# Keys of batches 3 to 7 projected by float32r parts in the full array, with the list of works searched anew

## The chip, the cores and the metric

The kernel runs on one core of one Trainium2 chip. The metric is the device time of one execution in microseconds (us); lower is better. Engines are named as the profile names them: PE (TensorE, matrix products; PEld its weight loads), DVE (VectorE), ACT (ScalarE), POOL (GpSimd), SP (SyncE, whose queue issues the DMAs).

## What is computed

Linear attention with positive random features, and then one feed-forward layer pair over its output. Inputs are q, k, v of 8 batches, 8 heads, 576 tokens, head size 64, and omega of 128 x 64, all float32.

```python
def phi(x):                                   # x already scaled by D ** -0.25
    proj = np.einsum('bhsd,md->bhsm', x, omega)
    h = proj - np.sum(x * x, axis=-1, keepdims=True) / 2.0
    h = h - np.max(h, axis=-1, keepdims=True)
    return np.exp(h) / np.sqrt(m)
q_p, k_p = phi(q_s), phi(k_s)
kv = np.einsum('bhsm,bhsd->bhmd', k_p, v)
z = np.sum(k_p, axis=2)
num = np.einsum('bhsm,bhmd->bhsd', q_p, kv)
attn = num / (np.einsum('bhsm,bhm->bhs', q_p, z)[..., None] + 1e-06)
x = attn.transpose(0, 2, 1, 3).reshape(4608, 512)
h = x @ w_in                                  # 512 x 2048
g = np.maximum(h, 0.0) + np.log1p(np.exp(-np.abs(h)))
out = g @ w_out                               # 2048 x 512
```

## The kernel before, in words

The heads of a batch are handled in two groups of four ("quads"; the names carry batch, quad and first token tile, so `xk_5_0_0` holds keys of batch 5, quad 0, tiles 0 and 1). A quad's 576 tokens come in units: tiles 0 and 1, tiles 2 and 3 (128 tokens each), and a tail of 64 tokens. `plan_unit` describes the work of one unit of queries or keys: a DMA brings it in twice (transposed, `raw`, and by rows, `nat`), the rows are squared and summed (`squares`, `norms`), `raw` is projected on omega, the maximum over the features is taken, and the exponent is written to the tile `phk` or `phq`.

There are two ways to project. In the plain one (`project`, line 590) a token tile takes two float32 products, one for each half of the 128 partitions (two heads stand above one another, 64 partitions each); the profile shows each as two PE instructions of 64x128, so a unit of two tiles, four pairs of heads, is 16 instructions. The maximum (`maxima`, line 640) and the exponent (`exponent`, line 660) read the PSUM result itself. In the split one (`high` line 604, `low` line 608, `product` line 615) the tile is taken apart into two float32r values, a rounded one and what is left; both stand above one another in the tile `sp`, so that all 128 partitions are used, and one product against `omr`, which holds omega's two parts side by side (256 columns), gives all that is wanted. Its two column halves are then added: `first` (line 625) copies one from PSUM to `phk`, `second` (line 628) adds the other; `all_maxima` (line 632) and `exponents` (line 637) work on `phk` in SBUF.

Which way a unit goes is decided by `if q.b < SPLIT[...]`: before, the queries and the 64-token tails of batches 2 to 7 are split, and the keys of all batches are plain (the limit for keys is 9, and there are 8 batches).

The feed-forward part runs beside this, in blocks of 512 tokens (the first two of 256): for each of 16 slices of the hidden layer, twelve products into a PSUM bank `h` (lines 1149 to 1151), softplus in three ACT steps and one DVE step (lines 1155 to 1164), the split of the result into float32r parts `gh` and `gl` (lines 1168, 1172), and twelve products into the output banks `acc` (lines 1209 to 1211). The last two blocks are computed together with fewer products (line 1483).

The order of everything is written out by hand: `do` collects works with what they wait for and which buffers they take and give, `in_order` goes through the table `ORDER`, and each engine then executes its works in that order. An entry says which work comes next and on which of its engines it runs, where it has two (DVE or POOL for `low`, ACT or DVE for `high` and `first`). The planner's costs in `in_order`, `change` and `dma` pick among free buffers, and where they show PE idle, `with_fill` puts products that nobody reads (line 1665). The buffer `x` (raw units) and the buffer `sp` exist once each, for queries and keys together; two PSUM banks (`at`) take the projections of batches 2 to 7.

Of the kernel before, what the change touches and what calls it, by code (L numbers as in the profile page):

```python
# [19 lines left out]
P = 128  # L20
# [14 lines left out]
START = {"SP": 0.6, "ACT": 2.1, "PE": 3.4}  # L35
SLOW = 6.8
# [281 lines left out]
def change(old, new):  # L318

    if old == new:  # L320
        return 0.0
    return {("r", None): 0.2, ("c", None): 0.07, (None, "r"): 0.32, (None, "c"): 0.275}.get((old, new), 0.185)
# [1450 lines left out]
```

## Time and profile before

| | |
|---|---|
| time, median of 3 runs | 1002.87 us (1000.95 to 1003.2) |
| time of the profiled execution | 1000.96 us |
| its span, first to last instruction | 999.2 us |
| PE busy | 983.9 us, 98% of the span |
| DVE busy | 782.6 us, 78% |
| ACT busy | 662.6 us, 66% |
| POOL busy | 239.3 us, 24% |
| plain projections of keys, line 590 | 532 PE instructions, 42.4 us |
| split projections, line 615 | 242 PE instructions, 32.5 and 8.1 us |

A row of a timeline gives the start, the time taken, the engine, the line, the operation, the tiles written and read, the shapes and how many instructions were merged into it; in brackets stands how long the engine had been idle, and what ended that. PE's matmuls overlap in these rows: what a product costs is read from one start to the next, not from its own duration.

### The profile page before, as it was taken

To read this page: it belongs to the slowest core of one execution; us is meant where nothing else is said; L and a number is where in the kernel's file an instruction comes from. 1 tells how busy PE (TensorE), PEld (TensorE's weight loads), DVE (VectorE), ACT (ScalarE), POOL (GpSimd) and SP (SyncE) were. 2 spreads that over 40 slices of the span, in tenths; PEclk is the share of its full clock that TensorE was granted. 3 is DMA by queue.
4 is the path that set the end of the run, shared out by engine and by line. 5 is a ranking of instruction groups with operands and counts; after the bars stand their busy time and mean duration, and the time that the engine had idled before them with its cause. 6 is when DMAs were issued, how large, how long until landed. Compare 5 with 4: busy or idle time off the path is not lost.

```text
span 999.2 us, 17174 instructions
## 1 busy us (share of the span) xinstructions
PE 983.9 (98%) x5721; PEld 805.7 (81%) x5721; DVE 782.6 (78%) x2072; ACT 662.6 (66%) x1621; POOL 239.3 (24%) x220
## 2 busy tenths in 40 slices
PE   9899999999999999999999999999999999999998
PEld 8778888787878877887878787878788778788886
DVE  7999987788888887878788877877788757998710
ACT  7999986667666675756666766767666635766610
POOL 2353232102313122222232221413121221111100
PEclk9999999999999999999999999999999999999999
DMA  9965445343343424352433334333433131000002
GB/s 313 374 229 182 125 151 140 116 121 95 119 127 114 133 78 143 106 150 77 120 105 112 106 98 148 101 109 119 109 121 118 54 103 42 1 1 1 1 11 74
DMA packets 65920, 113.56 MB, mean 114 GB/s; under 512 B 18444, under 2 KB 39080, under 8 KB 65832
## 3 DMA queue, kind: packets, MB, share of 16 engines
q1 hardware_dynamic: 65672, 112.34, 35.6%
q8 instruction: 45, 0.74, 0.3%
q14 instruction: 43, 0.35, 0.1%
q10 hardware_dynamic: 160, 0.13, 0.1%
HBM read 85.41 MB, written 27.03 MB: 113 GB/s over the span
## 4 chain that ended last, share of the span: by engine, by line
PE 89%; ACT 6%; DVE 4%; issue 1%; DMA 0%; SPq 0%; DVEq 0%; ACTq 0%
PE acc L1209 13%; PE acc L1210 12%; PE acc L1211 12%; PE h L1149 10%; PE h L1150 9%; PE h L1151 9%; PE ppk L590 3%; PE xp L1078 3%; PE kt L756 3%; PE pb L1483 2%; PE ppq L615 2%; PE pc L1483 2%; PE pa L1483 1%; PE h L1326 1%; PE h L1324 1%
## 5 line engine op out<-in xcount | busy, mean ns | idle before, releaser
L1209 PE MATMUL acc<-wo,gh 128*128 128x512 f32 x512 | 204.7, 400 | 0.5 <-DVE xq L925 0.4
L1210 PE MATMUL acc<-wo,gh 128*128 128x512 f32 x512 | 200.3, 391 | 0.0
L1211 PE MATMUL acc<-wo,gl 128*128 128x512 f32 x512 | 199.7, 390 | 0.0
L1149 PE MATMUL h<-xh,wi 128*128 128x512 f32 (+1 forms) x512 | 189.7, 370 | 1.9 <-DVE u L1164 1.8
L1150 PE MATMUL h<-xl,wi 128*128 128x512 f32 (+1 forms) x512 | 186.4, 364 | 0.0
L1151 PE MATMUL h<-xh,wi 128*128 128x512 f32 (+1 forms) x512 | 185.8, 363 | 0.0
L1172 POOL TENSOR_TENSOR gl<-u,gh 128x512 fp32r<-128x512 f32 (+1 forms) x63 | 80.5, 1277 | 221.8 <-ACT gh L1168 119.5
L1209 PEld LDWEIGHTS acc<-wo,gh 128*128 128x128 f32 x512 | 96.2, 188 | 27.6 <-issue 7.3
L1155 ACT ACTIVATE u<-h 128x512 f32<-128x512 f32 (+1 forms) x128 | 70.2, 549 | 68.1 <-PE h L1151 56.2
L1149 PEld LDWEIGHTS h<-xh,wi 128*128 128x128 f32 x512 | 96.5, 189 | 21.3 <-DVE u L1164 3.4
L1211 PEld LDWEIGHTS acc<-wo,gl 128*128 128x128 f32 x512 | 96.1, 188 | 20.7
L1210 PEld LDWEIGHTS acc<-wo,gh 128*128 128x128 f32 x512 | 96.4, 188 | 16.9
L1151 PEld LDWEIGHTS h<-xh,wi 128*128 128x128 f32 x512 | 96.5, 188 | 15.6
L1150 PEld LDWEIGHTS h<-xl,wi 128*128 128x128 f32 x512 | 96.7, 189 | 14.0 <-DVE xl L1098 0.2
L1164 DVE SCALAR_TENSOR_TENSOR u<-h,u 128x512 f32<-128x512 f32 (+1 forms) x128 | 78.6, 616 | 25.2 <-ACT u L1161 24.7
L988 DVE CUSTOM_DVE_ANT_0 junk<-phq,zb 128x128 bf16<-128x128 f32 (+1 forms) x228 | 74.6, 327 | 13.2
L1158 ACT ACTIVATE u<-u 128x512 f32<-128x512 f32 (+1 forms) x128 | 74.4, 582 | 2.9
L1161 ACT ACTIVATE u<-u 128x512 f32<-128x512 f32 (+1 forms) x128 | 74.2, 582 | 2.6
L660 ACT ACTIVATE phk<-ppk,smk 128x128 f32<-128x128 f32 x230 | 63.5, 381 | 14.7 <-DVE smk L652 14.6
L637 ACT ACTIVATE phq<-phq,smq 128x128 f32<-128x128 f32 x194 | 60.7, 391 | 12.1 <-DVE smq L652 12.0
L1168 ACT CAST gh<-u 128x512 fp32r<-128x512 f32 (+1 forms) x87 | 48.8, 563 | 24.3 <-DVE u L1164 11.2
L997 POOL TENSOR_TENSOR phq<-phq,dnq 128x512 f32<-128x512 f32 (+1 forms) x31 | 33.8, 1095 | 127.2 <-DVE dnq L993 103.6
(220 smaller groups left out, 1857.9 us busy)
## 6 DMA issues: line engine op xcount, KB each, us to landing
xk<-kx SPq DMA_DIRECT2D x28, 512.0 KB, 4.0
xq<-qx SPq DMA_DIRECT2D x28, 512.0 KB, 3.6
fdq<-flq SPq DMA_DIRECT2D x28, 512.0 KB, 2.8
qq<-fdq SPq DMA_DIRECT2D x112, 128.0 KB, 3.0
rawi<-wi SPq DMA_DIRECT2D x16, 512.0 KB, 6.9
rawo<-wo SPq DMA_DIRECT2D x16, 512.0 KB, 8.2
out<-o SPq DMA_DIRECT2D x32, 256.0 KB, 2.1
v<-vv SPq DMA_DIRECT2D x14, 576.0 KB, 3.8
```

The source lines that it names most:

```text
L988: nc.vector.tensor_tensor_reduce(jk[r, c % jk.shape[1]], ph[r, c], q.zb[r, h], 1.0, 1e-6, ALU.mult, ALU.add, dn[r, 0, c : c + 1])
L1149: nc.tensor.matmul(b["h"], wh, xh[:, cc, t], start=cc == 0, stop=False)
L1150: nc.tensor.matmul(b["h"], wh, xl[:, cc, t], start=False, stop=False)
L1151: nc.tensor.matmul(b["h"], wl, xh[:, cc, t], start=False, stop=cc == NCC - 1)
L1155: nc.scalar.activation(b["u"], b["h"], AF.Abs)
L1158: nc.scalar.activation(b["u"], b["u"], AF.Exp, scale=-1.0)
L1161: nc.scalar.activation(b["u"], b["u"], AF.Ln, bias=1.0)
L1164: nc.vector.scalar_tensor_tensor(b["u"], b["h"], 0.0, b["u"], ALU.max, ALU.add)
L1172: (nc.vector if e == "DVE" else nc.gpsimd).tensor_tensor(b["gl"], b["u"], b["gh"].bitcast(F32), ALU.subtract)
L1209: nc.tensor.matmul(dst, gh, w2[fc][:, 0, c], start=start, stop=False, **kw)
L1210: nc.tensor.matmul(dst, gh, w2[fc][:, 1, c], start=False, stop=False, **kw)
L1211: nc.tensor.matmul(dst, gl, w2[fc][:, 0, c], start=False, stop=stop, **kw)
```

## The change

The limit for keys falls from 9 to 3, so the units of two full tiles of keys of batches 3 to 7 (five batches, two quads, two units: 20 units) take the split way that queries already take. The first batch's keys come in with fewer DMAs: for token tiles 1 to 4 the key columns and the value columns that stand behind them are one transfer of 772 columns instead of two of 512 (256 for the last tile) and 260. Four of the planner's costs are changed, and the table `ORDER` is replaced as a whole.

```diff
-START = {"SP": 0.6, "ACT": 2.1, "PE": 3.4}
-SLOW = 6.8
+START = {"SP": 0.65, "ACT": 2.1, "PE": 3.4}
+SLOW = 7.2
...
 ORDER = (
-    384, 386, 410, 434, 458, 482, 391, 506, 530, 554, 578, 604, 630, 388, 463, 414, 666, 394, 418, 442, 466, 702, 436,
...
+    384, 394, 386, 410, 434, 456, 415, 418, 440, 462, 437, 390, 392, 396, 398, 416, 400, 402, 478, 500, 522, 544,
...
-    return {("r", None): 0.2, ("c", None): 0.07, (None, "r"): 0.32, (None, "c"): 0.275}.get((old, new), 0.185)
+    return {("r", None): 0.08, ("c", None): 0, (None, "r"): 0.4, (None, "c"): 0.29}.get((old, new), 0.185)
...
-        return max(0.55 * n, size / 400e3)
+        return max(0.55 * n, 0.11 + size / 450e3)
...
-        alone = early and kind == "k" and not u and not q.qd
+        apart = early and kind == "k" and not u
+        alone = apart and not q.qd
         b = {}
+
+        cols = w if alone else 2 * w if kind == "q" or apart or not early else VW
...
-                b["cols"](slice(0, w if alone else 2 * w))
+                b["cols"](slice(0, cols))
...
-        if early and kind == "k":
-            b["lv"] = do("SP", dma(P * 4 * (VW - UW)), lambda: b["cols"](slice(UW, VW)), behind=ld, delay=DL)
+        b["lv"] = do("SP", dma(P * 4 * (VW - UW)), lambda: b["cols"](slice(UW, VW)), behind=ld, delay=DL) if apart else None
...
-        if q.b < SPLIT["t" if tail else kind]:
+        if q.b < (3 if kind == "k" and not tail else 2):
```

On PE, at the first keys of batch 5, the order before has a plain projection of tiles 0 and 1 as one group between two pieces of the feed-forward part (`acc` and `h`):

```order
L1211 MATMUL acc_4_0_5049<-wo4_901,gl_4_4_5308 128x512
L590 MATMUL ppk_5_0_0_0_5337<-omf_82,xk_5_0_0_5185 128x128
L590 MATMUL ppk_5_0_0_1_5338<-omf_82,xk_5_0_0_5185 128x128
L590 MATMUL ppk_5_0_0_0_5337<-omf_82,xk_5_0_0_5185 128x128
L590 MATMUL ppk_5_0_0_1_5338<-omf_82,xk_5_0_0_5185 128x128
L590 MATMUL ppk_5_0_0_0_5337<-omf_82,xk_5_0_0_5185 128x128
L590 MATMUL ppk_5_0_0_1_5338<-omf_82,xk_5_0_0_5185 128x128
L590 MATMUL ppk_5_0_0_0_5337<-omf_82,xk_5_0_0_5185 128x128
L590 MATMUL ppk_5_0_0_1_5338<-omf_82,xk_5_0_0_5185 128x128
L1149 MATMUL h_4_7_5351<-xh_79,wi7_998 128x512
L1150 MATMUL h_4_7_5351<-xl_80,wi7_998 128x512
L1151 MATMUL h_4_7_5351<-xh_79,wi7_998 128x512
```

and now, at the same keys (lines have moved down by 18 or 19):

```order
L1229 MATMUL acc_4_1_5133<-wo4_884,gl_4_4_5368 128x512
L634 MATMUL ppk_5_0_0_0_5449<-omr_86,spk_5_0_0_5352 128x256 x2
L634 MATMUL ppk_5_0_0_1_5454<-omr_86,spk_5_0_0_5352 128x256 x2
L1167 MATMUL h_4_7_5460<-xh_79,wi7_971 128x512
L1168 MATMUL h_4_7_5460<-xl_80,wi7_971 128x512
L1169 MATMUL h_4_7_5460<-xh_79,wi7_971 128x512
L1167 MATMUL h_4_7_5460<-xh_79,wi7_971 128x512
L1168 MATMUL h_4_7_5460<-xl_80,wi7_971 128x512
L1169 MATMUL h_4_7_5460<-xh_79,wi7_971 128x512
L634 MATMUL ppk_5_0_0_2_5478<-omr_86,spk_5_0_0_5352 128x256 x2
L634 MATMUL ppk_5_0_0_3_5484<-omr_86,spk_5_0_0_5352 128x256 x2
L1167 MATMUL h_4_7_5460<-xh_79,wi7_971 128x512
```

The eight plain products in one place (16 instructions in the profile) have become two groups of four products of 256 columns, with six products of the feed-forward part between them. Over the whole program `ppk` now has 106 plain products instead of 266 and 208 split ones instead of 48.

On DVE, the same unit has these rows before: the sum of squares (line 580), the two maxima from PSUM (line 640), and two short steps.

```order
L1022 STREAM_TRANSPOSE flq_4_0_2_5358<-phq_4_0_2_0_5104 128x8x4x32
L580 TENSOR_REDUCE smk_5_0_0_5378<-xk_5_0_0_5185 128x8
L640 TENSOR_REDUCE smk_5_0_0_5378<-ppk_5_0_0_0_5337 128x4
L640 TENSOR_REDUCE smk_5_0_0_5378<-ppk_5_0_0_1_5338 128x4
L647 SCALAR_TENSOR_TENSOR smk_5_0_0_5378<-smk_5_0_0_5378 128x8
L652 SCALAR_TENSOR_TENSOR smk_5_0_0_5378<-smk_5_0_0_5378 128x8
L1022 STREAM_TRANSPOSE flq_4_0_4_5399<-phk_4_1_4_1_5218 128x2x4x32
L1172 TENSOR_TENSOR gl_4_5_5404<-u_4_5_5265,gh_4_5_5370 128x512
```

Now DVE makes the low parts ahead of the products (line 627), and the sum of squares follows:

```order
L851 TENSOR_TENSOR s_4_1_5236<-s_4_1_5236,phk_4_1_4_0_5289 64x256 x2
L627 TENSOR_TENSOR spk_5_0_0_5352<-xk_5_0_0_5307,spk_5_0_0_5352 64x512 x2
L1006 ISA junk_78,dnq_4_0_2_0_5342<-phq_4_0_2_0_5238,zb_4_0_4833 128x128
L1006 ISA dnq_4_0_2_0_5342 128x1
L599 TENSOR_REDUCE smk_5_0_0_5359<-xk_5_0_0_5307 128x8
L1190 TENSOR_TENSOR gl_4_4_5368<-u_4_4_5280,gh_4_4_5366 128x512
```

and further down the four additions (line 647) and one maximum over all eight rows (line 651):

```order
L647 TENSOR_TENSOR phk_5_0_0_0_5475<-ppk_5_0_0_0_5449,phk_5_0_0_0_5475 128x256
L647 TENSOR_TENSOR phk_5_0_0_0_5475<-ppk_5_0_0_1_5454,phk_5_0_0_0_5475 128x256
L623 CAST spq_4_1_0_5487<-xq_4_1_0_5467 64x512
L647 TENSOR_TENSOR phk_5_0_0_0_5475<-ppk_5_0_0_2_5478,phk_5_0_0_0_5475 128x256
L647 TENSOR_TENSOR phk_5_0_0_0_5475<-ppk_5_0_0_3_5484,phk_5_0_0_0_5475 128x256
L1011 RECIPROCAL dnq_4_0_4_0_5382<-dnq_4_0_4_0_5382 128x2
L1040 STREAM_TRANSPOSE flq_4_0_2_5502<-phq_4_0_2_0_5238 128x8x4x32
L651 TENSOR_REDUCE smk_5_0_0_5359<-phk_5_0_0_0_5475 128x8
L1190 TENSOR_TENSOR gl_4_6_5518<-u_4_6_5437,gh_4_6_5516 128x512
L1015 TENSOR_TENSOR phk_4_1_4_1_5290<-phk_4_1_4_1_5290,dnq_4_0_4_0_5382 128x256
```

Two maxima have become two subtractions, four additions and one longer maximum; the units of keys now take turns with those of the queries, as `spq_4_1_0` between two additions shows. Counted over the program, DVE has 80 more additions for keys (line 647), 40 fewer maxima from PSUM and 20 more from SBUF, 28 more subtractions for keys and 13 fewer for queries; ACT has 69 more copies of `phk` (line 644), 32 more casts for keys and 11 more for queries (line 623); POOL has 12 more subtractions for keys and 13 more for queries.

On SP, the first weights now come after ten rows of the first batch's loads instead of eighteen; from token tile 1 on, a key transfer is half as large again, the separate transfers of 260 columns are gone but for tile 0, and the queries' loads follow the keys'.

## Rows read from the trace of the kernel before

**Rows 1.** The page: its busy times and the clock granted to PE.

```profile
PE 983.9 (98%) x5721; PEld 805.7 (81%) x5721; DVE 782.6 (78%) x2072; ACT 662.6 (66%) x1621; POOL 239.3 (24%) x220
...
PEclk9999999999999999999999999999999999999999
```

**Rows 2.** Busy time by stretch: start and end, then its length, engines, clock, DMA.

```profile
0.00:50.00 50.00, 45.04 (x384) 39.77 (x384) 43.47 (x155) 41.53 (x122) 15.65 (x24) 1.00 0.93 344
50.00:100.00 50.00, 46.77 (x383) 40.02 (x383) 49.00 (x123) 48.24 (x134) 23.85 (x18) 1.00 0.60 206
100.00:150.00 50.00, 49.29 (x382) 43.33 (x380) 44.91 (x135) 44.18 (x125) 15.74 (x16) 1.00 0.45 137
200.00:750.00 550.00, 549.37 (x3123) 442.53 (x3123) 441.07 (x1199) 367.19 (x896) 134.03 (x117) 1.00 0.38 114
```

**Rows 3.** The waits of PE: us in total, times, longest.

```profile
PE ppk L590 <- DMA xk<-k: 0.9, 2, 0.7
```

**Rows 4.** Timeline of PE around one plain unit, the first keys of batch 5.

```profile
434.10 0.39 PE L1211 MATMUL acc<-wo,gl 128*128 128x512 f32 x1
434.41 1.16 PE L590 MATMUL ppk<-omf,xk 64*128 64x128 f32 x16
435.50 0.50 PE L1149 MATMUL h<-xh,wi 128*128 128x512 f32 x1
435.84 0.39 PE L1150 MATMUL h<-xl,wi 128*128 128x512 f32 x1
```

**Rows 5.** Line 590 alone in the stretch of the 20 units.

```profile
200.00:750.00 550.00, 23.68 (x320) 19.70 (x320) 1.00 0.38 114
```

**Rows 6.** Timeline of all engines where split products run.

```profile
467.39 0.39 PE L1211 MATMUL acc<-wo,gl 128*128 128x512 f32 x1
...
467.62 0.64 PE L615 MATMUL ppq<-omr,spq 128*128 128x256 f32 x4
...
468.09 0.40 PE L1149 MATMUL h<-xh,wi 128*128 128x512 f32 x1
...
468.32 0.40 PE L1150 MATMUL h<-xl,wi 128*128 128x512 f32 x1
...
470.39 2.70 POOL L829 TENSOR_TENSOR s<-s,phk 128x512 f32<-128x512 f32 x2
...
470.77 2.61 DVE L608 TENSOR_TENSOR spk<-xk,spk 64x256 fp32r<-64x256 f32 x2
...
472.69 0.28 PE L615 MATMUL ppk<-omr,spk 128*128 128x256 f32 x1
...
473.44 0.38 PE L615 MATMUL ppk<-omr,spk 128*128 128x256 f32 x1 [0.47 <-DVE spk L608]
...
474.30 0.39 PE L1209 MATMUL acc<-wo,gh 128*128 128x512 f32 x1
```

**Rows 7.** Line 608: count, then ns min/median/max, first and last start.

```profile
L608 DVE TENSOR_TENSOR spk<-xk,spk x9: 418/420/1393, 150.8 to 743.7; 64x256 fp32r<-64x256 f32 x9
```

**Rows 8.** Timeline of PE at one more plain unit.

```profile
270.03 1.60 PE L590 MATMUL ppk<-omf,xk 64*128 64x128 f32 x16
```

**Rows 9.** Timeline of PE at 786 us.

```profile
786.12 0.47 PE L615 MATMUL ppq<-omr,spq 128*128 128x256 f32 x2 [0.57 <-DVE phq L628]
```

**Rows 10.** Groups by form: busy, mean ns of one, idle before.

```profile
L640 DVE TENSOR_REDUCE smk<-ppk 128x4 f32<-128x512 f32 x56 | 36.4, 682 | 9.2 <-PE ppk L590 8.7
...
L608 DVE TENSOR_TENSOR spq<-xq,spq 64x512 fp32r<-64x512 f32 x42 | 31.5, 749 | 3.0 <-ACT spq L604 1.9
...
L628 DVE TENSOR_TENSOR phk<-ppk,phk 128x256 f32<-128x256 f32 x24 | 9.4, 418 | 0.9 <-ACT phk L625 0.6
...
L632 DVE TENSOR_REDUCE smq<-phq 128x8 f32<-128x1024 f32 x24 | 29.2, 1217 | 0.6
...
L604 ACT CAST spq<-xq 64x512 fp32r<-64x512 f32 x28 | 17.3, 617 | 0.4
...
L625 ACT COPY phk<-ppk 128x256 f32<-128x256 f32 x17 | 5.8, 373 | 10.4 <-PE ppk L615 10.4
```

More of the change, by code (lines that the diff above doesn't have):

```diff
@@ L662, in plan_unit @@
         ld = do(
-            "SP", dma(P * 4 * (w if alone else 2 * w)) + (0.6 if early and u == q.qd == 1 else 0), load, behind=prev.get("load"),
+            "SP", dma(P * 4 * cols) + (0.7 if apart and q.qd else 0), load, behind=prev.get("load"),
             take=[("w" if early else "x", b, "x")], delay=DL, spare=2 if early else 0,
@@ L667, in plan_unit @@
         if alone:
-            prev["load"] = ln = do("SP", 0.75, lambda: b["cols"](slice(w, 2 * w)), behind=ld, delay=DL)
-        if early and kind == "k":
-            b["lv"] = do("SP", dma(P * 4 * (VW - UW)), lambda: b["cols"](slice(UW, VW)), behind=ld, delay=DL)
+            prev["load"] = ln = do("SP", 0.55, lambda: b["cols"](slice(w, 2 * w)), behind=ld, delay=DL)
+        b["lv"] = do("SP", dma(P * 4 * (VW - UW)), lambda: b["cols"](slice(UW, VW)), behind=ld, delay=DL) if apart else None
         s = do(("POOL", "ACT"), (pool(w), act(w)), squares, after=[ln])
```

491 rows, old and new, of the table ORDER are left out of this document.

## The prediction

> **What bounds the kernel now.** I read the page's busy times first [rows 1]: PE works for 98% of the span, at the full 2.4 GHz clock in every slice, and no other engine passes 78%. The stretches come next [rows 2]. In the first 50 us PE is idle for 5.0 us, in the second 50 for 3.2, in the third for 0.7; from 200 to 750 us, where all keys stand that change their way, it is idle for 0.6 of 550 us, with DVE at 441.07 / 550 = 80%, ACT at 67% and POOL at 24%. So in that stretch the time is PE's own work: what PE no longer has to do comes off the end one for one, as long as the other three still deliver in time. Busy time alone does not price a product, since matmuls overlap; so the third view is the timeline of PE, read from start to start.
>
> **The plain projection goes, 20 times.** The source has 5 batches, 2 quads and 2 full units each; line 590 shows x320 instructions in the stretch, 16 for each unit, so all 20 lie there [rows 5]. At one of them the last 512-column product ahead starts at 434.10 and the second one behind at 435.84, 1.74 us later [rows 4]. Without the group two products would have started in that time, 0.23 us each (467.39 to 467.62 in [rows 6]). The group costs 1.74 - 0.46 = 1.28 us. Some 0.2 us of it are the late starts at both edges (0.31 us ahead of the group and 0.34 behind the next product, where 0.23 is usual), which the full array does not show.
>
> **The split products come, 80 token tiles.** Two tiles in a row are four products of 256 columns: 467.39 to 468.32 is 0.93 us, less the same 0.46 is 0.47 us [rows 6]. A unit of four tiles takes 0.94 us. The order leaves most of them in such groups of two tiles, and a group by itself splits no further work. So a unit gives back 1.28 - 0.94 = 0.34 us, and 20 units 6.8 us. This is the one term that is nearly certain, since both kinds of group are in the trace of before, among the same neighbours.
>
> **What DVE, ACT and POOL get.** DVE: 80 additions at 418 ns are 33.4 us; 20 maxima over eight rows at 1217 ns are 24.3, against 40 maxima at 682 ns that go, 27.3; 28 subtractions for keys at 749 ns are 21.0, and 13 for queries that go to POOL are 9.7 less [rows 10]. Together +41.7 us, which lifts DVE from 80% to 483 / 550 = 88% of the stretch. ACT: 69 copies at 373 ns and 43 casts at 617 ns [rows 10] are 25.7 + 26.5 = 52.2 us, so 419 / 550 = 76%. POOL gets 25 subtractions more. All this lies beside PE's products; it costs nothing while the softplus steps and the queries' additions still come in time, and what they cost if they don't is the next term. A new wait comes with it: the buffer `sp` is one for queries and keys, so ACT's cast for the next unit waits for the last product of the one before, with softplus steps queued behind that cast on ACT; the order puts the casts behind such products.
>
> **Waits in the stretch.** Before, PE lost time there in two visible places: one plain group took 1.60 us instead of the usual 1.16, 0.44 lost [rows 8], and a run of split products, 472.69 to 474.30, took 1.61 where 0.47 is usual (467.62 to 468.09), 1.1 lost [rows 6]. A third stands just behind, 0.57 at 786.12 [rows 9]. That is 2.1 us, and as the whole order is new, those three go. How many come instead no row can say, so I bound it. The lower end is none at all, a gain of 2.1 us. The upper end is the rate of the stretch from 100 to 150 us, where DVE works for 44.9 of 50 us, 90%, and PE is idle for 0.71 [rows 2]: times 11 it is 7.8 us. DVE's 88% is near that row, but there ACT is at 88% too, and here at 76%; so I take 4.5 us, between the old 2.1 and that end, and keep both ends. Net: -2.4 us.
>
> **The start.** Key transfers of 772 columns bring 133 KB more each than those of 512, and at the 344 GB/s of the first 50 us [rows 2] that is 0.39 us; the sixth such transfer lands some 2.3 us later. PE waited 0.9 us in all for those keys [rows 3], so the third and fourth tile come 0.4 and 0.8 us later where PE is waiting. Against that there are eight DMAs fewer on SP's queue, the values land with the keys, and weights are asked for sooner; PE's 8.2 idle us of the first 100 are the room for a gain. I bound it by -2 and +2.3 and take 0. The last 150 us keep their work, and I take 0 there too.
>
> **The sum.** The profiled execution took 1000.96 us, 1.76 more than its span. 1000.96 - 6.8 - 2.1 + 4.5 = 996.6 us. That execution lies at the low end of the runs (median 1002.87, 1.9 higher), and which level the changed kernel's runs take is open; I put the forecast about midway, at 997.4 us.
>
> **A rule that speaks against it.** DVE and POOL disturb each other in this trace: while POOL makes two sums from 470.39 to 473.09, DVE's two subtractions of 64x256 take 2.61 us together [rows 6], where the median of that form is 420 ns and the longest 1393 [rows 7], and PE's next products then wait for them. The Trainium skill, SBUF — State Buffer, section "SBUF: two separate sides", says that a DVE operation with two SBUF inputs and a GpSimd operation that reads SBUF exclude each other for a whole instruction, since they share a pair of ports. By that rule every one of the added subtractions can be held or can hold; the trace agrees for the two above. What it would do here is the first rival.
>
> **Rivals.**
> 1. DVE's subtractions are held by POOL (slower). Place: the low parts of the keys, right ahead of PE's products. Price: 1.1 us of PE for one such event [rows 6]. The gain of 6.8 + 2.1 = 8.9 us is used up by eight of them, one in eight of the 66 subtractions that DVE will have (51 before [rows 7, 10], 28 more and 13 fewer); with ten, 1000.96 - 8.9 + 11 = 1003.1 us. For it: DVE and POOL both get more of this work, and at 98% DVE (49.0 of 50 us, from 50 to 100) PE loses 3.2 us in 50 [rows 2]. Against: before, one event in 51 such subtractions reached PE. 8%.
> 2. The start, or more waits, eat most of the gain: +2.3 us at the start and the upper 7.8 us of waits give 1000.96 - 8.9 + 7.8 + 2.3 = 1002.2 us, no change. For it: PE already waits for those keys [rows 3]. Against: most of the first 50 us' idle time is not charged to DMAs. 14%.
> 3. The other engines deliver as before and the new order leaves no more waits than the old one: 1000.96 - 6.8 = 994.2 us, and with none at all 992.1. For it: 24% of ACT and 12% of DVE stay free. 15%.
> 4. Leaving the row-packed form is a loss in itself: a product that is given up as one of two side by side would then take twice its packed group, 20 x 1.28 = 25.6 us more than before, so 1026.6 us. For it: the plain products do use 64 rows each [rows 4]. Against: split products fill all 128 rows and take 0.47 us for two tiles [rows 6]. 1%. The Trainium skill, TensorEngine Tiling (Array Packing), section "Theoretical Speedup", promises up to 2x from packing where a dimension is 64 or less; the rows do not bear that out against these products, whose two parts stand above one another.
>
> **How the numbers follow.** The forecast itself, 6.8 us less work and some two of them lost again, gets 62%: 994.5 to 1000 us. The range that should hold 8 in 10 runs from 993.5, inside rival 3, to 1001.5, inside rival 2. A change of 0.2%, 2.0 us, is about what a measurement of this kernel can tell. Faster by more than that are all but a hundredth of the forecast, rival 3 and a hundredth of rival 2: 0.77. Within it lie 0.10 of rival 2, 0.03 of rival 1 and a hundredth of the forecast: 0.14. Slower: what is left of rivals 1 and 2, and rival 4: 0.09.
>
> **What would show it.** Right: between 200 and 750 us line 590's successor has no keys left, runs of four split products cost 0.47 us from start to start, DVE is at 86 to 90% and ACT at 74 to 78%, and the same feed-forward product comes ever earlier than before, by some 0.3 us for each unit passed. PE's waits in the stretch then sum to 3 to 6 us, most of them ended by DVE. Wrong: products of the keys that wait for a low part again and again (rival 1), the first feed-forward product later than before by over 1 us (rival 2), or split products that cost more than 0.5 us for two tiles.

## The result, and the profile after

The changed kernel takes 1008.62 us (median of 4 runs, 1008.27 to 1010.17), the kernel before 1002.41 us beside it. The ratio is 1.0067, 95% interval 1.0049 to 1.0084: slower by 0.7%. The forecast was 997.4 us, and the range ended at 1001.5. The profiled execution took 1010.17 us, the longest of the four; its span is 1008.2 us. Lines have moved down by 18 or 19: `project` is 609, `high` 623, `low` 627, `product` 634, `second` 647; the feed-forward products are 1167 to 1169 and 1227 to 1229, the pair at the end is 1501.

The page after, its busy times, against [rows 1]:

```profile
PE 985.2 (98%) x5563; PEld 809.0 (80%) x5563; DVE 828.0 (82%) x2147; ACT 711.8 (71%) x1735; POOL 281.8 (28%) x251
```

The first and the last of the stretches of [rows 2]:

```profile
0.00:50.00 50.00, 44.68 (x348) 39.54 (x349) 40.28 (x141) 37.52 (x110) 15.19 (x23) 0.97 0.98 373
200.00:750.00 550.00, 543.95 (x2953) 441.20 (x2952) 473.03 (x1248) 416.18 (x1008) 177.31 (x149) 1.00 0.37 112
```

From 200 to 750 us DVE is at 473.03 / 550 = 86% and ACT at 76%, where 86 to 90% and 74 to 78% were said. PE is idle there for 6.0 us; before it was 0.6. The granted clock of the first stretch is 0.97, before 1.00.

The price of the split products is as forecast. A timeline of PE around two token tiles of keys:

```profile
455.61 0.39 PE L1169 MATMUL h<-xh,wi 128*128 128x512 f32 x1
455.84 0.64 PE L634 MATMUL ppk<-omr,spk 128*128 128x256 f32 x4
456.31 0.40 PE L1167 MATMUL h<-xh,wi 128*128 128x512 f32 x1
```

From 455.61 to 456.31 is 0.70, less one 512-column product (0.23) 0.47 us, the value read from [rows 6].

The start is one of two places where the time was lost. PE's timeline of the first 16 us after, and the first feed-forward product:

```profile
3.87 2.27 PE L609 MATMUL ppk<-omf,xk 64*128 64x128 f32 x16 [0.32 <-DMA xk<-k]
7.48 2.39 PE L609 MATMUL ppk<-omf,xk 64*128 64x128 f32 x16 [1.33 <-DMA xk<-k]
...
12.30 2.88 PE L1683 MATMUL fill<-ident 128*128 128x128 f32 x16
15.24 0.78 PE L609 MATMUL ppk<-omf,xk 64*128 64x128 f32 x8
...
44.47 0.39 PE L1167 MATMUL h<-xh,wi 128*128 128x256 f32 x1
```

and before:

```profile
5.68 2.93 PE L590 MATMUL ppk<-omf,xk 64*128 64x128 f32 x24 [0.72 <-DMA xk<-k]
...
40.40 0.37 PE L1149 MATMUL h<-xh,wi 128*128 128x256 f32 x1
```

The second batch of key products begins 1.8 us later (7.48 and 5.68), and the feed-forward part 4.1 us later. Around that, PE is at its lower clock of 1.2 GHz for a while (columns as in [rows 2]):

```profile
36.00:40.00 4.00, 2.89 (x30) 2.54 (x27) 3.97 (x12) 3.57 (x10) 1.38 (x3) 1.00 1.03 410
40.00:44.00 4.00, 2.90 (x24) 2.42 (x25) 3.93 (x15) 2.60 (x8) 1.27 (x1) 1.00 1.02 409
44.00:48.00 4.00, 4.00 (x25) 3.43 (x26) 3.97 (x16) 3.48 (x10) 1.28 (x1) 0.60 1.03 411
```

The granted clock is 0.60 from 44 to 48 us, after PE had worked for 2.89 and 2.90 of 4 us in the two slices before; in the kernel before it is 1.00 in all three.

The waits of PE from 200 to 850 us (us in total, times, longest):

```profile
PE ppk L634 <- DVE phq L647: 1.5, 3, 0.7
PE h L1167 <- DVE u L1182: 1.2, 2, 1.0
PE acc L1227 <- ACT o L1244: 1.2, 1, 1.2
PE xp L1096 <- DMA qq<-fdq: 1.1, 1, 1.1
PE ppk L634 <- ACT s L795: 0.4, 1, 0.4
PE ppq L634 <- DVE phq L647: 0.4, 1, 0.4
```

They stand at nine places from 485 us on, 5.8 us together; before, there were three in this stretch, 1.2 us together. At the end, the pair of last blocks waits twice for a softplus step, where before it waited once for 0.81 us:

```profile
875.89 0.50 PE L1501 MATMUL pb<-xh,t 128*128 128x512 f32 x1 [1.62 <-DVE hc L1534]
903.97 0.50 PE L1501 MATMUL pb<-xh,t 128*128 128x512 f32 x1 [0.60 <-DVE hc L1534]
```

With PE's rows read from start to start, the whole comes apart as follows, here with four of the kernels of the next section (us; the first three lines add up to the fourth):

| | before | after | e1 | e7 | e8 |
|---|---|---|---|---|---|
| first feed-forward product starts | 40.4 | 44.5 | 41.3 | 43.0 | 42.7 |
| PE's waits over 60 ns behind it | 6.6 | 13.1 | 11.3 | 7.4 | 7.9 |
| PE's rows, start to start, without these | 947.7 | 945.9 | 944.1 | 943.0 | 949.1 |
| last product starts | 994.7 | 1003.4 | 996.7 | 993.4 | 999.7 |
| span ends | 999.2 | 1008.2 | 1001.9 | 998.4 | 1004.5 |

After against before: +4.1 at the start, +6.5 in waits, -1.8 in PE's own rows, +0.3 behind the last product.

The prediction's sign that the same feed-forward product would come ever earlier held for half of the stretch. Counted product by product against the kernel before (means of 120), the feed-forward part is 5.6 us late near 200 us and 1.8 near 474; near 511 it is 4.3 late, and at the end 8.7. The gain came, and was lost again where the waits stand.

### The profile page after: what moved, and what is told of

It is laid out like the page before. It is cut to its first block, busy times and chain, and to the rows that moved or that the text cites. A ratio compares the mean times of both kernels' runs of the same rounds, so it can differ in the third digit from the quotient of the medians.

```text
span 1008.2 us, 17087 instructions
## 1 busy us (share of the span) xinstructions
PE 985.2 (98%) x5563; PEld 809.0 (80%) x5563; DVE 828.0 (82%) x2147; ACT 711.8 (71%) x1735; POOL 281.8 (28%) x251
## 5 line engine op out<-in xcount | busy, mean ns | idle before, releaser
L1190 POOL TENSOR_TENSOR gl<-u,gh 128x512 fp32r<-128x512 f32 (+1 forms) x71 | 86.2, 1214 | 227.3 <-ACT gh L1186 111.7
L1006 DVE CUSTOM_DVE_ANT_0 junk<-phq,zb 128x128 bf16<-128x128 f32 (+1 forms) x228 | 82.8, 363 | 10.8 <-ACT spk L623 0.2
L656 ACT ACTIVATE phk<-phk,smk 128x128 f32<-128x128 f32 x208 | 67.0, 394 | 5.7 <-DVE smk L671 5.6
L1015 POOL TENSOR_TENSOR phq<-phq,dnq 128x512 f32<-128x512 f32 (+1 forms) x34 | 37.7, 1117 | 82.4 <-DVE dnq L1011 49.3
L1186 ACT CAST gh<-u 128x512 fp32r<-128x512 f32 (+1 forms) x83 | 45.6, 552 | 12.6 <-PE acc L1228 6.5
```

Of the source, the lines that this page charges most:

```text
L656: nc.scalar.activation(x, x, AF.Exp, bias=b["sm"][:, 2, c : c + 1])
L1006: nc.vector.tensor_tensor_reduce(jk[r, c % jk.shape[1]], ph[r, c], q.zb[r, h], 1.0, 1e-6, ALU.mult, ALU.add, dn[r, 0, c : c + 1])
L1190: (nc.vector if e == "DVE" else nc.gpsimd).tensor_tensor(b["gl"], b["u"], b["gh"].bitcast(F32), ALU.subtract)
```

## The experiments

Ratios are those of the runs to runs of the kernel before on the same chip, with their 95% interval.

**e1: the start of before, then the changed order.** Against the kernel before; in `ORDER` the first 1103 entries stay, behind them the rest of the works stands in the changed kernel's order:

```diff
-        if q.b < SPLIT["t" if tail else kind]:
+        if q.b < (3 if kind == "k" and not tail else 2):
```

> The first 172 us (by the plan) stand as in the kernel before, with its separate loads of the value columns; behind that the works stand in the changed kernel's order, with the split keys of batches 3 to 7. Theory A (the changed kernel loses about 6 us ahead of its first feed-forward product and keeps that loss to the end): first layer-1 product at 40.4 us as before, not 44.5; no stretch at a lower clock; time 1002 to 1003.5. Rival B (PE waits for the same halves of the work later on, so that a start won is given back): first product at 40.4, but time 1006 to 1009.

Measured: 1004.3 us, ratio 1.0019 (1.0006 to 1.0032), first product at 41.3 us, clock 1.00 in every slice. That is 0.48% or 4.8 us better than the changed kernel, and 0.8 us short of theory A's band: the start cost some 5 us, and little of what was won there was given back. Theory A's first product, 40.4, came 0.9 us late. What is left is 4.6 us of waits from 200 to 850 us, at much the same places as after.

**e2: only the joint transfers.** Against the kernel before; the eight entries of the separate value loads go from `ORDER`:

```diff
-        alone = early and kind == "k" and not u and not q.qd
+        apart = early and kind == "k" and not u
+        alone = apart and not q.qd
+        cols = w if alone else 2 * w if kind == "q" or apart or not early else VW
...
-                b["cols"](slice(0, w if alone else 2 * w))
+                b["cols"](slice(0, cols))
...
-        if early and kind == "k":
+        b["lv"] = None
+        if apart:
```

> The kernel before with one edit: eight of its ten key loads bring all 772 columns at once; its order of works is kept otherwise, and its keys are projected as before. Theory A1 (the wide transfers are the cause at the start): second batch of key products at 7.0 to 7.5 us, not 5.7; first layer-1 product 2 to 4 us later than 40.4; time 1004 to 1006.5. Rival A2 (the new order and its fill are the cause, the wide transfers cost under 1 us): first product within 1 us of 40.4, time 1001.5 to 1003.5.

Measured: 1006.94 us, ratio 1.0041 (1.0028 to 1.0054). The first feed-forward product:

```profile
44.39 0.37 PE L1151 MATMUL h<-xh,wi 128*128 128x256 f32 x1
```

4.0 us later, and from there on each feed-forward product keeps a distance of 3.6 to 4.0 us to the kernel before, up to the last. So the joint transfers alone cost 4 us at the start, and nothing gives them back. The median of twelve runs says the same, 4.1 us, 0.4 above A1's band. Theory A1 had the place wrong, though: the second batch of key products began at 5.34 us, no later than before. It is the queries, behind the keys in the same queue, that come late: their first product starts at 24.96 us, before at 21.35.

**e3: the changed kernel with the transfers divided again.**

```diff
-        cols = w if alone else 2 * w if kind == "q" or apart or not early else VW
+        cols = w if alone else 2 * w
...
-        b["lv"] = do("SP", dma(P * 4 * (VW - UW)), lambda: b["cols"](slice(UW, VW)), behind=ld, delay=DL) if apart else None
+        b["lv"] = do("SP", dma(P * 4 * (VW - UW)), lambda: b["cols"](slice(UW, VW)), behind=ld, delay=DL) if early and kind == "k" else None
```

> The changed kernel with the 772-column transfers divided again into 512 and 260 columns, the second part issued eight transfers behind the first; its order is kept otherwise. Theory A1 (wide transfers): second batch of key products at 5.7 to 6.5 us, first layer-1 product at 41 to 42.5, time 1005 to 1007. Rival A2 (order and fill): first product at 43.5 to 45, time 1008 to 1009.5.

Measured: 1005.21 us, ratio 1.0028 (1.0017 to 1.0039), first product at 42.9 us, the second batch of key products at 5.14. The same transfers taken out of the changed kernel give back 0.39%, 3.9 us, in time: e2 from the other side. The first product, in the one profiled execution of each, moves by only 1.6 us, and 42.9 lies above A1's band. The slices at the lower clock stay (0.90 and 0.68 from 40 to 48 us), so that drop comes from the new order, not from the transfers.

**e4: less fill at the start.** Against the changed kernel, in `with_fill`:

```diff
-            n = int((t - last - (0.05 if t < 16 else 0.25)) / (0.43 if t < SLOW else 0.224)) if last is not None and t < until else 0
+            n = int((t - last - (0.05 if t < 16 else 0.25)) / (0.43 if t < 16 else 0.224)) if last is not None and t < until else 0
```

> The changed kernel with about half as many fill products between 7.2 and 16 us of the plan. Theory C (the fill was counted for PE at its full rate and ran at about half of it, so that it kept the key products of the third to fifth load waiting up to 4 us): the key products that began at 15.24 us begin by 12.5 to 13.5, first layer-1 product 1 to 3 us earlier than 44.5, time 1005.5 to 1007.5. Rival D (PE needs the fill to come to its full rate, so with less of it the products themselves run longer): first product at 44 to 47, time 1008.5 to 1011.

Measured: 1009.26 us, ratio 1.0075 (1.0052 to 1.0099), no better than the changed kernel, and with six runs from 1006.97 to 1015.19. Theory C falls. In the profiled execution, at 1013.23 us the second longest of the six, PE stayed at half its pace far longer:

```profile
17.45 1.30 PE L609 MATMUL ppk<-omf,xk 64*128 64x128 f32 x8
```

```profile
32.00:36.00 4.00, 4.00 (x26) 3.66 (x26) 0.80 (x3) 1.28 (x4) 1.84 (x2) 1.00 1.03 410
36.00:40.00 4.00, 4.00 (x38) 3.81 (x37) 4.00 (x13) 3.45 (x10) 1.62 (x2) 1.00 1.03 410
```

A key group takes 1.30 us there (0.78 at full pace), and 23 to 26 products fit into 4 us up to 36 us, 38 behind it; the first feed-forward product came at 51.2 us, well above theory D's 44 to 47, while the median time lies in D's band. With less fill PE came to its pace later in this execution, as theory D has it; since that moment moves between executions of one start as well (e10), one profile does not show that the fill decides it.

**e5 and e6: the order behind the start searched again, with split keys and with plain ones.** e5 against e1, e6 against the kernel before: `ORDER` alone, from entry 1096 on. Its first line in e5:

```diff
-    1094, 1092, 2146, 2696, 1632, 1946, 2150, 1096, 1098, 1100, 1102, 2166, 1617, 1635, 2646, 2648, 2169, 2650, 2652,
+    1094, 1092, 2146, 2696, 1632, 1100, 1634, 1617, 2646, 1096, 2694, 2648, 2650, 2698, 1637, 1102, 2166, 2169, 2173,
```

> The works of the kernel with the old start (split keys of batches 3 to 7, first 170 us as before); behind that start the works are ordered again, by a search that also weighs DVE works 2.5% longer, waits for another engine 5% longer and single works longer by a few per cent. Theory F (the waits of the changed kernel behind 400 us and at its end come from an order with no slack, not from the work that the split keys add): PE waits 2 us or less between 200 and 850 us, not 4.6 to 5.9; about 1.2 us at the end; time 995 to 998.5, faster than before. Rival G (DVE at 85% and its collisions with POOL make such waits in any order): waits of 4 to 6 us in the stretch, time 1002 to 1005.

> The kernel before, its works and loads unchanged, with its order behind the first 170 us searched in the same way. Theory F: its own order had this slack already, so time 1000.5 to 1003, no change. If it comes out 4 us or more faster than the kernel before, the search and not the split keys is what e5 gains by.

Measured: e5 1004.7 us, ratio 1.0023 (1.0014 to 1.0032); e6 1006.51 us, 1.0038 (1.0025 to 1.005). Both times miss theory F. The waits come near it, 2.2 us between 200 and 850 us in e5 where F's bound was 2, and its last product starts at 993.5 us, 1.3 earlier than in the kernel before. SP's queue behind that product shows where it went:

```profile
994.49 1.20 SPq L1256 DMA_DIRECT2D out<-o  x2
995.79 0.54 SPq L1252 DMA_DIRECT2D out<-o  x1
996.41 1.11 SPq L1256 DMA_DIRECT2D out<-o  x2
997.58 0.57 SPq L1252 DMA_DIRECT2D out<-o  x1
998.27 2.58 SPq L1256 DMA_DIRECT2D out<-o  x4
```

Ten stores at some 0.6 us each, one behind the other; the span ends 10.2 us after the last product (in e6 9.1), before 4.5. The search had asked for the last product alone, and left stores that were long ready to the end of the queue.

**e7 and e8: the same with the last stores counted.** `ORDER` alone again; its first line in e7:

```diff
-    1094, 1092, 2146, 2696, 1632, 1946, 2150, 1096, 1098, 1100, 1102, 2166, 1617, 1635, 2646, 2648, 2169, 2650, 2652,
+    1094, 1092, 2146, 2696, 1096, 1632, 1635, 1100, 2646, 1617, 1102, 2166, 2694, 1618, 2648, 1636, 2169, 2698, 1620,
```

> As e5, but the search now counts the landing of the last stores too; in e5 the last product ended at 993.5 us, 1.3 earlier than in the kernel before, and ten stores were issued behind it, so that the span ended 10.2 us after the last product instead of 4.5. Theory F2 (the order was the cause of the waits, and e5 lost its gain to those stores alone): last product at 992 to 995 us, span 4.5 to 5.5 us longer, PE waits of 2 us or less between 200 and 850 us, time 997 to 1000.5. Rival G2 (work that the split keys add costs as much as they save, in any order): 1002 to 1005.

> As e6 (keys plain, as in the kernel before), with the same search as e7. Theory F2: 1000.5 to 1003.5, within 0.2% of the kernel before, since its order had the slack already; e7 is then 2.5 to 5 us faster than this one by its keys alone. If e8 is as fast as e7, the split keys give nothing.

Measured: e7 999.39 us, ratio 0.9967 (0.9954 to 0.998), faster than both kernels; e8 1005.83 us, 1.0037 (1.0022 to 1.0051). e7's stretch with the 20 units and its waits from 200 to 850 us:

```profile
200.00:750.00 550.00, 547.73 (x2976) 444.83 (x2975) 480.38 (x1268) 406.93 (x989) 192.37 (x170) 1.00 0.39 114
```

```profile
PE ppq L632 <- DVE phk L645: 1.6, 1, 1.6
PE ppk L632 <- DVE phk L645: 0.3, 1, 0.3
PE h L1166 <- DVE u L1181: 0.2, 1, 0.2
```

With the same split keys as after, and DVE even busier (480.38 us, 87%), PE waits 2.1 us instead of 5.8. In e1, which has the same works and the same start as e7 in another order, it waits 4.6: theory F2 stands for the waits (its bound was 2), and the order decides them. By their ratios e7 is 0.52%, 5.2 us, faster than e1. Against e8, which has the same start and the same search and differs by the keys alone, e7 is 0.9967 / 1.0037 = 0.993, 7.0 us faster; by the two intervals that is good to some 2 us. How much comes out depends on the orders that a search finds: e5 and e6, which also differ by the keys alone, are 1.5 us apart in time and 3.0 in their last product, and against the kernel before e7 gains some 3 us. Theory F2 did not foresee that e8 would be 3.7 us slower than the kernel before. Its first product comes 2.3 us later, and behind it both its waits and its rows are 1.3 to 1.4 us longer (table); the rows are longer by what its waits cost beside their idle time (see the next section).

**e9: the values in small transfers, in the order of the joint ones.** Against the kernel before, `ORDER` alone: the eight entries of the value loads stand right behind their key loads.

```diff
-    384, 386, 410, 434, 458, 482, 391, 506, 530, 554, 578, 604, 630, 388, 463, 414, 666, 394, 418, 442, 466, 702, 436,
+    384, 386, 410, 434, 436, 458, 460, 482, 484, 391, 506, 508, 530, 532, 554, 556, 578, 580, 604, 606, 630, 388, 463,
```

> The kernel before with its separate transfers (512 and 260 columns) kept, but the 260 value columns of each of the same eight key loads now issued right behind the 512, so that the bytes come in the same order as with the joint transfers of e2. Theory H (what costs 4 us is that 1.06 MB of values come in ahead of the queries on a busy DMA): first layer-1 product 2 to 4 us later than in the kernel before, time 1004.5 to 1007.5. Rival I (the size of one transfer is what costs, its order does not): first product as in the kernel before, time 1001.5 to 1003.5.

Measured: 1007.9 us, ratio 1.0053 (1.0041 to 1.0065).

```profile
46.63 0.37 PE L1149 MATMUL h<-xh,wi 128*128 128x256 f32 x1
```

6.2 us later than before, and the queries' first product at 27.21 us. So it is not the size of a transfer: 8 x 133 KB = 1.06 MB of values, moved ahead of the queries, take 3.1 us at the 344 GB/s of [rows 2], on DMAs that are busy for 0.96 of the first 44 us in the kernel before. That estimate is below both delays, 4.0 and 6.2 us; what adds the rest is open. Rival I falls. Both the time, 5.4 us over the kernel before, and the first product lie above H's bands: in small transfers the same bytes cost no less than in joint ones, and whether they cost more is open, since the intervals of e2 and e9 overlap.

**e10: the kernel before once more.** No edit.

> The kernel before once more, unchanged, to see how far the start of one program moves from one profiled execution to another. If its first layer-1 product comes at 41 to 43 us rather than at 40.4, then 1 to 2.5 us of the later starts of e1 and e5 to e8, which keep that start, are no effect of their edits.

Measured: one run of 1001.59 us, first feed-forward product at 40.95 us. So the start moves by 0.6 us between these two executions. It explains 0.6 of the later starts of e5 to e8, and not their 1.7 to 2.6 us. So a single profiled start can be off by up to 2.6 us against a kernel with the same start; for the delays of e2 and e9 the medians of twelve and of six runs, 4.1 and 5.4 us, are the firmer figures, though a shift that stays with a program would stand in them too; e3, with 3.9 us from the other side, speaks against much of that. The twelve fill products ahead of the third key batch show the difference, first e10, then e7:

```profile
9.12 1.58 PE L1665 MATMUL fill<-ident 128*128 128x128 f32 x12 [0.96 <-issue]
10.76 0.79 PE L590 MATMUL ppk<-omf,xk 64*128 64x128 f32 x8
```

```profile
9.24 2.90 PE L1682 MATMUL fill<-ident 128*128 128x128 f32 x12 [0.49 <-issue]
12.20 1.29 PE L607 MATMUL ppk<-omf,xk 64*128 64x128 f32 x8
```

The same products in the same place take 1.58 us in one execution and 2.90 in another: in e10 PE is at its full pace by 9.12 us, in e7 not before 13.4. What decides that, these runs don't tell.

**e11: DVE beside POOL.** Against the kernel before, behind the last work:

```diff
...
+        def dve(k):
+            for _ in range(k):
+                nc.vector.tensor_tensor(pg, pa, pc, ALU.subtract)
+            for _ in range(k):
+                nc.vector.tensor_copy(pg, pa)
+            for _ in range(k):
+                nc.vector.tensor_tensor(pc[:, :256], ps_[:, :256], pc[:, :256], ALU.add)
+
+        dve(6)
...
+        for _ in range(14):
+            nc.gpsimd.tensor_tensor(pe, pe, pd, ALU.add)
...
+        dve(6)
```

> The kernel before with a measurement behind its last product, of no use for its output (the time, some 30 us longer, is not to be compared): six DVE subtractions 128x512 from SBUF, six copies 128x512, six additions 128x256 of PSUM and SBUF, first alone, then the same beside fourteen POOL additions 128x512. Theory J (a DVE operation with two inputs from SBUF and a POOL operation wait for each other, those with one input from SBUF do not): subtractions 0.66 to 0.70 us alone and 1.4 to 1.8 us beside POOL (1.04 us each there), copies 0.42 and additions 0.42 in both. Rival K (they only share bandwidth): all three kinds 10 to 40% longer beside POOL.

Measured (timeline, rows of DVE and POOL in the order of their starts):

```profile
1000.84 4.26 DVE L1685 TENSOR_TENSOR probeg<-probeph,probeph 128x512 fp32r<-128x512 f32 x6
1005.13 2.73 DVE L1687 CAST probeg<-probeph 128x512 fp32r<-128x512 f32 x6
1007.78 2.71 DVE L1689 TENSOR_TENSOR probeph<-probep,probeph 128x256 f32<-128x256 f32 x6
...
1011.35 20.83 POOL L1694 TENSOR_TENSOR probex.0_10751<-probex.0_10751,probeph 128x512 f32<-128x512 f32 x14 [53.48 <-DVE marks L1695]
1011.68 8.30 DVE L1685 TENSOR_TENSOR probeg<-probeph,probeph 128x512 fp32r<-128x512 f32 x5
1020.01 8.37 DVE L1687 CAST probeg<-probeph 128x512 fp32r<-128x512 f32 x6
1028.30 2.71 DVE L1689 TENSOR_TENSOR probeph<-probep,probeph 128x256 f32<-128x256 f32 x6
```

A subtraction goes from 4.26 / 6 = 0.71 us to 8.30 / 5 = 1.66; theory J holds for it. It fails for the casts, which go from 0.455 to 1.40 us, and K fails for all: the additions that read PSUM take 2.71 us both times, with POOL at work. The starts of subtractions and casts alternate one for one with those of POOL's additions, 1.67 us apart with subtractions and 1.40 with casts; POOL's own additions take 1.59 and 1.32 us there.

## Why the prediction was wrong

Two steps failed, by about the same amount: the start, taken as 0, and the waits, taken as a net loss of 2.4 us. By the ratios of whole runs, the old start gives back 4.8 us (after to e1), and another order behind it 5.2 us more (e1 to e7). With both, e7's 999.39 us lies inside the range that was forecast for the changed kernel.

**The products of the 20 units: right.** 0.47 us for two tiles was 0.47. From start to start, all rows of key products take 35.8 us instead of 38.4, and the 512-column products beside plain groups (counted behind 100 us) come 0.7 us late in all instead of 4.7. Together that is 6.5 us, forecast 6.8. But in the whole PE's rows became only 1.8 us shorter, because a wait costs more than its idle time:

```profile
743.87 0.39 PE L1229 MATMUL acc<-wo,gl 128*128 128x512 f32 x1
745.44 0.50 PE L1227 MATMUL acc<-wo,gh 128*128 128x512 f32 x1 [1.18 <-ACT o L1244]
745.78 0.40 PE L1228 MATMUL acc<-wo,gh 128*128 128x512 f32 x1
```

The product ahead of this wait takes 745.44 - 743.87 - 1.18 = 0.39 us, and the first behind it 0.34, where 0.23 is usual. Such edges of waits add 2.5 us to the rows of the changed kernel behind 100 us, 0.35 before, 1.1 in e7 and 1.7 in e8. Some 2 us more stand in the stretch at the lower clock: the layer-1 products (`h`) take 337.6 us, 336.3 in e1, and the transposes of the first batch 4.7, 3.7 in e1.

**The start: failed.** It was bounded by -2 and +2.3 us and taken as 0; it was +4.1 in the profile, +4.1 in time for the joint transfers alone (e2) and 4.8 for the whole start (e1). The 0.39 us for each transfer was not far off: e2's 4.0 us are 0.5 for each of the eight. But I charged them only to the keys for which PE was seen waiting [rows 3] and only up to the sixth, and let the rest hide. The queries follow in the same queue, and the first feed-forward product needs them: on DMAs that are busy all that time, the bytes ahead of the last input of that product count, 3.1 us of values by the estimate at e9, whatever PE waits for. The rows of the stretch showed it: DMA share 0.93 [rows 2]. Rival 2 had the place, at 2.3 us and 14%, but by way of the keys and not of the queries. The lower clock comes on top, by the new order (e3).

**Waits in the stretch: failed.** 4.5 us were taken, and PE was idle for 6.0 from 200 to 750 us, inside the bound of 7.8. The old waits that go were 2.1 us by [rows 6, 8, 9], and by the same reading of rows 1.2 before 850. The net was +4.8 instead of +2.4. I took the rate from a stretch with DVE at 90%, as if the load made the waits. e7 has more load and little more than a third of the waits of after. So the order decides, and the busy share does not show it; that it is the slack which the order leaves to each product's last input is my reading, which no run measures by itself. I also left out that each wait lengthens the products at its edges, 2.2 us more than before in all. "Most of them ended by DVE" was half right: 3.1 of 5.8 us.

**The end: failed.** It was taken as 0, since the work stays. Its order did not: the pair at the end waited 2.2 us instead of 0.8. It is the order here too: all of PE's waits behind 850 us come to 2.5 us in after, 1.0 before and 0.7 in e7.

**DVE held by POOL (rival 1): real, at another place.** e11 shows it at full size. None of the waits listed is ended by a long subtraction. But the multiply-and-reduce step (line 1006, also with two inputs from SBUF, 0.29 us as a median) is held as well, and it stands ahead of the softplus step that ended the longest wait put down to DVE:

```profile
513.76 2.73 POOL L627 TENSOR_TENSOR spq<-xq,spq 64x512 fp32r<-64x512 f32 x2 [4.99 <-ACT spq L623]
...
514.23 1.04 DVE L1006 CUSTOM_DVE_ANT_0 junk<-phq,zb 128x128 bf16<-128x128 f32 x1
...
515.31 1.32 DVE L1006 CUSTOM_DVE_ANT_0 junk<-phq,zb 128x128 bf16<-128x128 f32 x1
...
518.04 0.68 DVE L1182 SCALAR_TENSOR_TENSOR u<-h,u 128x512 f32<-128x512 f32 x1
...
518.77 0.50 PE L1167 MATMUL h<-xh,wi 128*128 128x512 f32 x1 [1.01 <-DVE u L1182]
```

These two steps lose 1.8 us while POOL makes two subtractions, and PE waits 1.0 us. Long steps of this kind stand on DVE shortly ahead of four of the nine waits, 2.8 of 5.8 us. From 200 to 850 us there are 21 that take over 0.6 us, 18.8 us beyond the median, all with POOL at work; before there were 8, 6.4 us. So the split keys do make POOL hold DVE more often. e7 has 18 of them, 16.9 us, and few waits: whether they reach PE is again a matter of the order. How much of the waits would go without them, no run shows.

The rule of the Trainium skill (SBUF — State Buffer, section "SBUF: two separate sides") names a second half that I left out: it also counts DVE operations in a 2-port mode. The casts of e11, 0.455 to 1.40 us, agree with that, though no run shows that they run in such a mode, and the additions from PSUM, unchanged, agree with its limit to SBUF.

**The sum, with what was measured in place of the terms:** 994.7 + 4.1 (start) + 6.5 (waits) - 1.8 (PE's rows) = 1003.5 us for the last product; it started at 1003.4.

## What to carry to other kernels

A transfer that is moved ahead of others is paid by the last input of the first long stage, not by the instruction that waits in the profile: add up the bytes in front of that input, and divide by the rate while the DMAs are full (here that gave 3.1 us, and 4.0 and 6.2 were measured). When an order is replaced as a whole, the saving that it was made for and the slack that it lost are two different things; keep the old start, compare with a control that has the new order without the change, and count what ends last, stores included. Busy shares tell whether an engine can deliver, and not whether it delivers in time. A wait costs its idle time and the slower products at its edges.

## What the runs showed of the hardware that I had not expected

A DVE cast from SBUF to SBUF waits for POOL as a subtraction does (0.455 us alone, 1.40 beside POOL's additions), though it has one input; an addition of PSUM and SBUF does not (0.45 both times). A wait of PE cost 0.27 us beside its idle time, 0.16 in the product ahead of it and 0.11 in the first behind it (after, 743 to 746 us). At the start, the same twelve products took 1.58, 2.04 (e1) and 2.90 us in different executions, with a granted clock that reads 1.00 in all of them, and with half the fill PE stayed at half pace until 36 us (e4). Two slices with PE at work for 2.9 of 4 us were followed by one at 0.60 of the clock (after, 44 to 48 us).
